# Transposing gathered rows of a mixture of experts on two 64-row tiles, up to four units at a time

## The chip, the cores and the metric

The kernel runs on one core of one Trainium2 chip. The metric is the device time of one launch in microseconds (us). The engines are named as the profile names them: PE is TensorE, DVE VectorE, ACT ScalarE, POOL GpSimd and SP SyncE.

## What is computed

Linear attention feeds a mixture of experts:

```python
def phi(x):
    proj = np.einsum('bhsd,df->bhsf', x, w_phi)
    proj = proj - np.max(np.abs(proj), axis=-1, keepdims=True)
    return np.concatenate([np.exp(proj), np.exp(-proj)], axis=-1)
kv = np.einsum('bhsf,bhsd->bhfd', k_p, v)
z = np.sum(k_p, axis=2)
num = np.einsum('bhsf,bhfd->bhsd', q_p, kv)
den = np.einsum('bhsf,bhf->bhs', q_p, z)[..., None] + 1e-06
...
e = fresh_e if s == 0 or local_gate[b, s] < 0.5 else prev_e
h = np.maximum(x[b, s] @ w1[e], 0.0)
out[b, s] = p[e] * (h @ w2[e])
```

There are 8 batches, 8 heads, 576 positions and 64 numbers a head; `num / den` of the 8 heads side by side is the row x of 512 numbers of a token. For each of the 4608 tokens a gate picks one of 8 experts (or keeps that of the token ahead of it), and the expert is two layers, 512 to 1024 with a relu and 1024 to 512, scaled by the gate's probability p. All inputs are fp32.

## The kernel before

Up to about 290 us the kernel does the attention, batch after batch, and the gates. Rows x are written to a DRAM buffer. PE works in this stage on 64 rows or 64 columns of its array at a time, and transposes with `halves` (line 290): two transposes of 64 rows each, on row tiles 0 and 64, into two banks.

A plan is then made on DVE, POOL and PE from the counts of tokens per expert: which tokens go together. A **unit** is up to 128 tokens of one expert. A **slot** is a few units of one expert that share one load of its weights: two early slots e0 and e1 of three units, made of the tokens known early, then four quads q0 to q3 (four units), four trips t0 to t3 (three), one pair p0 (two), and shared slots d0, d1 with one unit of two experts, 64 tokens each. `moe` (line 1229) sets the order q0, t0, d0, q1, t1, q2, d1, t2, q3, t3, p0. A guarded loop behind them is not run with these inputs.

A slot's work, `slots` (line 1165), runs like this. `gather_x` (line 998) fetches each unit's 128 rows with an indirect DMA on POOL's queue into one of six buffers `xg`. `tokens` (line 1015) returns one step for each unit: four 128x128 transposes on PE (line 1034) into one PSUM bank `tr`, a copy on ACT that rounds to the first half `xhi` (line 1043), and a subtraction on DVE that leaves the second half `xlo` (line 1044). Those steps are called from within the second layer of the slot ahead, one after the first matmuls of each of its units and one after the third (lines 1145 on); a shared slot has them between its four first-layer quarters. The first layer (`layer1`, line 1071) takes eight tiles of 128 hidden numbers, each four times three matmuls (`three`, lines 1048 to 1050: hi*hi, lo*hi, hi*lo) into a PSUM tile `l1` of three buffers; relu on ACT writes `hh` (line 1093) and DVE writes what is left over, `hl` (line 1094). The second layer (line 1132) takes 24 matmuls a unit into `l2`; DVE scales to `y` (line 1153) and POOL scatters the rows to the output (line 1156). The plan's later steps (`fetch`, lines 715 to 753, with the gather `lr` by POOL at line 736, for which DVE first makes `p_rim` at line 722, and the transpose on PE at line 753) run beside e0 and e1.

A shared slot (`layer1_one`, line 1100) has tokens as rows: four quarters of 256 hidden numbers, each a matmul pair on 64 columns per expert (line 1061), a relu into `hs` (line 1122), and `turn`, two transposes with one copy (lines 1109 to 1116), four times. `hs` then stands transposed in `hh`.

Weights come by DMA on SP's queue into five raw buffers; `split` (line 947) rounds them on ACT (`whi`, line 956, 128x1024) and subtracts on DVE (`wlo`, line 959). Every engine takes its instructions in the order written; the scheduler interleaves the lists by its own estimates, except that `past` keeps a split behind the last relu. PSUM has eight banks: from e1's end on `tr` and `l2` have two each (psr), a third `tr` one (psm4), and `l1` three (psl). In the early slots `tr` is taken from the attention's pool pskv.

Of the kernel before, what the change touches and what calls it, by code (L numbers as in the profile page):

```python
# [7 lines left out]
F32 = mybir.dt.float32  # L8
F32R = mybir.dt.float32r
# [5 lines left out]
PSUM = bass.MemoryType.PSUM  # L15
# [40 lines left out]
class Kernel:  # L56
# [9 lines left out]
    def run(self):  # L66
        nc, tc, A = self.nc, self.tc, self.A
        act, dve = self.act, self.dve
        with ExitStack() as root:
# [6 lines left out]
            first = self.const.tile([128, 256], F32, name="first")  # L76
# [32 lines left out]
            n = NBP * NHP * NC  # L109
# [19 lines left out]
            p = n // 2  # L129
# [777 lines left out]
    def open_main(self, root):  # L907

        self.mxt = self.mkpool(root, "moe_x2", 1, "right")
        self.w_right = self.mkpool(root, "moe_wr", WR, "right")  # L910
        self.mx2 = self.mkpool(root, "moe_h2", 2, "right")
        self.psm4 = self.mkpool(root, "moe_ps1", 1, "right", PSUM)
        self.psl = self.mkpool(root, "moe_ps2", 3, "right", PSUM)
        self.wphases = [(self.moe_early, WE), (self.w_right, WR)]

    def open_rest(self, root):
        self.w_left = self.mkpool(root, "moe_wl", WL, "left")
        self.ml1 = self.mkpool(root, "moe_l1", 1, "left")
        self.psr = self.mkpool(root, "moe_ps3", 2, "left", PSUM)
        self.wphases = [(self.moe_early, WE), (self.w_right, WR), (self.w_left, WL)]  # L920

    def wpool(self):
# [80 lines left out]
            self.pool.indirect_dma_start(x, None, self.xs[0:s["rows"], :], bass.IndirectOffsetOnAxis(s["tok"][:, u:u + 1], 0))  # L1003
            s["xg"].append(x)

    def turned(self):

        self.trn = getattr(self, "trn", 0) + 1
        if hasattr(self, "psr") and self.trn % 3:
            return self.psr.tile([128, 4, 128], F32, name="tr")  # L1010
        if not hasattr(self, "psr") and self.trn % 3 != 2:
            return self.pskv.tile([128, 4, 128], F32, name="tr", tag="kvp")
        return self.psm4.tile([128, 4, 128], F32, name="tr")

    def tokens(self, s, late=False):

        pe, n = self.pe, s["n"]
        if "xg" not in s:
            self.gather_x(s)

        def step(k):
            if k == 0:
                p = self.mxt if n > 1 else self.ml1
                s["x"] = [p.tile([128, 4, n * 128], F32R, name=x + "1" * (n == 1)) for x in ("xhi", "xlo")]
            hi, lo = s["x"]
            t = self.turned()
            with ExitStack() as st:
                if late:
                    st.enter_context(self.here())
                elif s is self.eslots[0]:  # L1030
                    st.enter_context(self.tc.high_priority())
                    st.enter_context(self.tc.issue_after(self.last_turn.ins))
                for d in range(4):
                    pe.transpose(t[:, d, :], s["xg"][k][:, d * 128:d * 128 + 128], self.ident)
            self.parts(s, hi, lo, slice(k * 128, k * 128 + 128), t)
        return [lambda k=k: step(k) for k in range(n)]

    def parts(self, s, hi, lo, o, t):

        if len(s["ei"]) == 2:  # L1040
            self.act.copy(hi[:, :, o].bitcast(F32), t)
        else:
            self.act.copy(hi[:, :, o], t)
            self.dve.tensor_sub(lo[:, :, o], t, hi[:, :, o].bitcast(F32))  # L1044

    def three(self, o, ah, al, bh, bl, first, last):
        mm = self.pe.matmul
# [52 lines left out]
    def layer1_one(self, s, between):  # L1100

        pe, act = self.pe, self.act
        xh, xl = s["x"]
        hh, hl = s["h"] = self.hidden(1)
        hs = self.ml1.tile([128, 1024], F32, name="hs", bufs=1)
        x = slice(0, 128)

        def turn(q):
            tt = self.turned()
            for j in (0, 1):  # L1110
                f = q * 2 + j
                pe.transpose(tt[:, j, :], hs[:, f * 128:f * 128 + 128], self.ident)
            hc = slice(q * 2, q * 2 + 2)
            self.parts(s, hh[:, hc], hl[:, hc], x, tt[:, 0:2])
        for q in range(4):
            t = self.psl.tile([128, 256], F32, name="l1")
            for d in range(4):
                self.both(s, q, t, xh[:, d, x], xl[:, d, x], slice(d * 256, d * 256 + 256), d == 0, d == 3)
                if d == 0 and q == 3:
                    turn(0)  # L1120
                    turn(1)
            act.activation(hs[:, q * 256:(q + 1) * 256], t, AF.Relu)
# [42 lines left out]
    def slots(self, order, held=None, soon=(), later=()):  # L1165
        first = order[0]
        if "x" not in first:
            for f in self.tokens(first):
                f()
        self.held = first.get("asked", len(first.get("w", ())))  # L1170
        self.coming, self.loaded = list(order), getattr(self, "loaded", [])
        self.marks = {}
        for i, s in enumerate(order):
            while s.get("asked", len(s.get("w", ()))) < 8:
                self.spare()
            self.need(s, 4)
            new = order[i + 1] if i + 1 < len(order) else None
            between = []
            for x in order[i + 1:i + 3 if new and len(new["ei"]) == 2 and s["n"] > 1 else i + 2]:
                if "x" not in x:  # L1180
                    between += self.tokens(x, bool(soon) and i == 0)
# [142 lines left out]
```

## Time and profile before

| what | us |
| --- | --- |
| median of 3 runs | 763.56 (762.89 to 764.04) |
| profiled execution | 755.65 |
| its span, first to last instruction | 753.9 |
| clock granted to TensorE, share of full | 0.999 |

Rows of the timeline have the start, the busy time, the engine, the line, the operation, output from inputs and shapes; "xN" are N instructions in a row, and in brackets stands how long the engine was idle ahead of it and what released it. Rows of the grouped views have the number of instructions, their busy time in us and the mean of one in ns, then the idle time ahead of them. A row of the waits has the waiting operation, what it waited for, the total, the count and the longest. PE's matmuls overlap their neighbours, so the distance between two starts says what one costs.

### The profile page before, as it was taken

The page shows a single profiled execution, that of the slowest core. Times are in us where ns is not written, and L with a number is a line of the kernel's source. Part 1 is how long each engine was busy: PE and PEld are TensorE (multiplying, and loading weights), DVE is VectorE, ACT ScalarE, POOL GpSimd, SP SyncE. Part 2 cuts the span into 40 slices and gives each one's busy share as a digit, 9 for nine tenths or more (in the row PEclk, how much of TensorE's full clock was granted, in tenths as well). Part 3 has the DMA queues.
Part 4 walks back from the last instruction along what each step waited for, and adds up shares of the span by engine and source line. Part 5 has one row for each costly group of instructions (what it writes and reads, how often), then busy time and mean ns, then how long its engine had stood idle before and what let it go on. Part 6 is the DMA issues. An engine that isn't in the chain of part 4 may idle for free. (4 is left out here: it accounts for less than half of the span.)

```text
span 753.9 us, 21898 instructions
## 1 busy us (share of the span) xinstructions
PE 728.9 (97%) x9319; PEld 632.8 (84%) x9319; DVE 451.9 (60%) x828; ACT 341.6 (45%) x648; POOL 182.1 (24%) x306
## 2 busy tenths in 40 slices
PE   7999999999998999999999999999999999999996
PEld 6999989989897888888788975889888778888995
DVE  5888888789887886674545245435522554443512
ACT  5766657666676673323343234333312444241301
POOL 0210103410374574443302041021302202101011
PEclk9999999999999999999999999999999999999999
DMA  7755545454666741154806977245486565432110
GB/s 215 247 160 141 155 123 149 138 151 130 212 202 179 229 127 54 56 178 148 314 35 248 393 248 262 83 156 193 142 289 237 162 225 168 140 125 98 57 39 29
DMA packets 66100, 125.04 MB, mean 166 GB/s; under 512 B 7220, under 2 KB 45300, under 8 KB 65950
## 3 DMA queue, kind: packets, MB, share of 16 engines
q1 hardware_dynamic: 57808, 101.03, 41.8%
q0 software_dynamic: 8016, 22.51, 8.7%
q8 instruction: 74, 1.21, 0.7%
q14 instruction: 26, 0.21, 0.1%
q10 hardware_dynamic: 176, 0.07, 0.0%
HBM read 102.05 MB, written 22.06 MB: 165 GB/s over the span
## 5 line engine op out<-in xcount | busy, mean ns | idle before, releaser
L1093 ACT ACTIVATE hh<-l 128x384 fp32r<-128x384 f32 (+1 forms) x84 | 45.2, 538 | 191.6 <-PE l L1050 191.6
L956 ACT CAST whi<-wraw 128x1024 fp32r<-128x1024 f32 x88 | 91.2, 1048 | 74.8 <-PE l L1050 42.4
L1049 PE MATMUL l<-xlo,whi 128*128 128x384 f32 (+2 forms) x352 | 123.6, 351 | 0.9 <-DVE xlo L1044 0.9
L1048 PE MATMUL l<-xhi,whi 128*128 128x384 f32 (+2 forms) x352 | 124.1, 353 | 0.0
L1050 PE MATMUL l<-xhi,wlo 128*128 128x384 f32 (+2 forms) x352 | 123.5, 351 | 0.0
L1094 DVE SCALAR_TENSOR_TENSOR hl<-l,hh 128x384 fp32r<-128x384 f32 (+1 forms) x84 | 51.6, 614 | 117.3 <-ACT hh L1093 117.2
L1048 PE MATMUL l<-whi,hh 128*128 128x512 f32 x288 | 116.8, 406 | 0.6 <-DVE y L1153 0.6
L1050 PE MATMUL l<-whi,hl 128*128 128x512 f32 x288 | 113.8, 395 | 0.0
L1049 PE MATMUL l<-wlo,hh 128*128 128x512 f32 x288 | 113.7, 395 | 0.0
L959 DVE TENSOR_TENSOR wlo<-wraw,whi 128x1024 fp32r<-128x1024 f32 x80 | 96.7, 1222 | 25.4 <-ACT whi L956 25.4
L285 ACT ACTIVATE kp<-sb 128x512 f32<-128x512 f32 x144 | 83.5, 625 | 58.7 <-DVE sb L281 56.9
L279 DVE TENSOR_REDUCE m<-pj 128x8 f32<-128x1024 f32 x72 | 87.8, 1219 | 34.0 <-PE pj L276 32.2
L276 PE MATMUL pj<-first,kq 64*128 64x128 f32 x1152 | 85.3, 289 | 7.6 <-DMA kq<-in_kqT 4.1
L281 DVE TENSOR_TENSOR sb<-pj,m 128x1024 f32<-128x1024 f32 x72 | 88.1, 1223 | 3.5
L309 ACT ACTIVATE qp<-pj 128x512 f32<-128x512 f32 x144 | 79.7, 594 | 23.1 <-PE pj L294 10.8
L404 PE MATMUL nm<-kvs,qp 128*64 128x74 f32 x2304 | 86.9, 228 | 1.4 <-ACT kvs L384 1.3
L276 PEld LDWEIGHTS pj<-first,kq 64*128 64x128 f32 x1152 | 71.5, 191 | 14.7 <-ACT ks L373 5.5
L404 PEld LDWEIGHTS nm<-kvs,qp 128*64 128x64 f32 x2304 | 79.5, 136 | 2.2 <-ACT kvs L384 1.7
L326 PE MATMUL kvp<-v,kp 128*64 128x65 f32 x2048 | 77.5, 225 | 1.3 <-issue 0.6
L1156 POOL DMA_INDIRECT out<-y,p_tokm x30 | 35.9, 1198 | 174.7 <-DVE y L1153 159.4
L1048 PEld LDWEIGHTS l<-xhi,whi 128*128 128x128 f32 x352 | 66.2, 188 | 7.5 <-issue 1.6
L326 PEld LDWEIGHTS kvp<-v,kp 128*64 128x64 f32 x2048 | 67.0, 137 | 5.7 <-ACT kp L285 1.8
(222 smaller groups left out, 923.8 us busy)
## 6 DMA issues: line engine op xcount, KB each, us to landing
wraw<-in_w1h SPq DMA_DIRECT2D x44, 512.0 KB, 5.0
wraw<-in_w2h SPq DMA_DIRECT2D x44, 512.0 KB, 5.1
kq<-in_kqT SPq DMA_DIRECT2D x47, 384.0 KB, 4.0
v<-in_va SPq DMA_DIRECT2D x48, 195.0 KB, 3.6
xs<-xo SPq DMA_DIRECT2D x48, 128.0 KB, 2.8
whi<-in_w1h SPq DMA_DIRECT2D x8, 512.0 KB
wlo<-in_w1h SPq DMA_DIRECT2D x8, 512.0 KB, 4.8
whi<-in_w2h SPq DMA_DIRECT2D x8, 512.0 KB
```

The source lines that it names most:

```text
L276: self.last_pe = self.pe.matmul(t[:, h, i % 2, j, :], kq[r, j, s], self.w2[r], start=True, stop=True)
L279: dve.tensor_reduce(m, f, AX.X, ALU.max, apply_absolute_value=True)
L281: self.last_dve = dve.tensor_sub(sb.rearrange("p h c j f -> p (h c j) f"), f, m.unsqueeze(2).broadcast_to([128, 8, 128]))
L285: self.last_act = act.activation(kp[:, :, :, sg, :].rearrange("p c h f -> p h c f"), sb[:, :, :, 0], AF.Exp, scale=1.0 - 2 * sg)
L309: self.act.activation(qp[:, sg].rearrange("p h (c r k) -> p (h c) r k", c=2, r=2), src, AF.Exp, scale=1.0 - 2 * sg)
L326: self.pe.matmul(t[r, sg, h], kp[:, h, sg, r], v[:, h], start=first and sg + h == 0, stop=last and sg + h == 2)
L404: self.last_num = self.pe.matmul(e["t"][r, c - c0, k], self.ch[i]["qp"][:, sg, h, q0 + r.start:q0 + r.stop], kvs[:, sg, k], start=sg == 0, ...
L956: self.act.copy(hi, raw)
L959: (low or self.dve).tensor_sub(lo[:, c], raw[:, c], hi.bitcast(F32)[:, c])
L1048: mm(o, ah, bh, start=first, stop=False)
L1049: mm(o, ah, bl, start=False, stop=False)
L1050: self.last_pe = mm(o, al, bh, start=False, stop=last)
```

## The change

Row tiles: where `turned` gave one bank for four 128x128 transposes, `halfbanks` gives two banks, and `rows` does eight transposes of 64 rows by 128 columns each, alternately on row tile 0 and row tile 64, one bank for each. `unrow` copies both banks with one ACT copy and one DVE subtraction of 512 columns.

Groups: `tokens` now takes the list of slots and returns steps of four units, in order (two where `late`, for e1 and q0). All transposes of a step stand next to each other on PE, then follow its copies. So e1 has a group of two and a single, q0 two pairs, t0 three, d0 with q1's first three units four, q1's last unit one, t1 three, q2 four, d1 with t2 four, q3 four, t3 three, p0 two. e0 and the single of e1 keep 128x128 transposes (`whole`). In the early slots a pair of units takes two separate banks of pskv, and `unrow` makes four copies and four subtractions of 64 tokens for two units.

Shared slots: `turn` does eight transposes of 64 rows for four tiles of `hs` and one copy of 512 columns, two times instead of four.

PSUM: the psm4 and psl pools are closed after e1, and `moe` runs with two `l1` buffers and with two `tr` tiles of two banks each, in psr and pst.

```diff
             def ahead():
-                m.append(self.tokens(self.by_size[4][0], True))
+                m.extend(self.tokens([self.by_size[4][0]], True))
...
-                       later=[[listed], [no, no] + [lambda k=k: m[0][k]() for k in range(4)]])
+                       later=[[listed], [no, no, lambda: m[0](), no, lambda: m[1]()]])
             back.close()
+            self.mid.close()
...
+        self.psl = self.mkpool(root, "moe_ps4", 2, "right", PSUM)
+        self.pst = self.mkpool(root, "moe_ps5", 1, "right", PSUM)
...
-    def turned(self):
+    def halfbanks(self):
 
         self.trn = getattr(self, "trn", 0) + 1
...
+        if not hasattr(self, "psr"):
+            return [self.pskv.tile([128, 512], F32, name="tr", tag="kvp") for _ in (0, 1)]
+        return (self.psr if self.trn % 2 else self.pst).tile([128, 2, 512], F32, name="tr", bufs=1)
...
+    def tokens(self, slots, late=False):
...
+        units, g = [(s, k) for s in slots for k in range(s["n"])], 2 if late else 4
+
+        def step(group):
+            if late and len(group) == 1:
+                self.whole(*group[0], True, self.here())
+                return
+            out = []
+            for n, (s, k) in enumerate(group):
+                if n % 2 == 0:
+                    t = self.halfbanks()
+                c = slice(n % 2 * 256, n % 2 * 256 + 256)
+                out.append((s, k, [x[:, c] for x in t] if isinstance(t, list) else t[:, :, c]))
+                with self.here() if late else nullcontext():
+                    self.rows(out[-1][2], s["xg"][k])
+            for s, k, t in out:
+                self.unrow(s, *self.into(s), k * 128, t)
+        return [lambda a=a: step(units[a:a + g]) for a in range(0, len(units), g)]
+
+    def rows(self, t, src):
+
+        for d in range(4):
+            for r in (0, 1):
+                k = slice(64 * r, 64 * r + 64)
+                o = t[r] if isinstance(t, list) else t[:, r]
+                self.pe.transpose(o[:, d * 64:d * 64 + 64], src[k, d * 128:d * 128 + 128], self.ident[k, k])
+
+    def unrow(self, s, hi, lo, at, t):
+
+        if isinstance(t, list):
+            for r in (0, 1):
+                self.parts(s, hi, lo, slice(at + 64 * r, at + 64 * r + 64), t[r].rearrange("p (d k) -> p d k", k=64))
+            return
+        hi, lo = [x[:, :, at:at + 128].rearrange("p d (r k) -> p d r k", r=2) for x in (hi, lo)]
+        self.parts(s, hi, lo, slice(0, 64), t.rearrange("p r (d k) -> p d r k", k=64))
...
         def turn(q):
-            tt = self.turned()
-            for j in (0, 1):
-                f = q * 2 + j
-                pe.transpose(tt[:, j, :], hs[:, f * 128:f * 128 + 128], self.ident)
-            hc = slice(q * 2, q * 2 + 2)
-            self.parts(s, hh[:, hc], hl[:, hc], x, tt[:, 0:2])
+            t = self.halfbanks()[:, :, 0:256]
+            self.rows(t, hs[:, q * 512:q * 512 + 512])
+            hc = slice(q * 4, q * 4 + 4)
+            self.unrow(s, hh[:, hc], hl[:, hc], 0, t)
...
                 if d == 0 and q == 3:
                     turn(0)
-                    turn(1)
...
-        def last():
-            turn(2)
-            turn(3)
-        return [last]
+        return [lambda: turn(1)]
```

What moves on the engines shows at three places. (Line numbers after the change are about 40 higher; `l_...` is a PSUM tile of a layer, with a number of its own.)

PE, the start of t0's second layer, before:

```order
L1048 MATMUL l_7603<-whi,hh 128x512
L1049 MATMUL l_7603<-wlo,hh 128x512
L1050 MATMUL l_7603<-whi,hl 128x512
L1034 MATMUL tr<-first,xg 128x128 x4
L1048 MATMUL l_7603<-whi,hh 128x512
L1049 MATMUL l_7603<-wlo,hh 128x512
L1050 MATMUL l_7603<-whi,hl 128x512
L1048 MATMUL l_7603<-whi,hh 128x512
L1049 MATMUL l_7603<-wlo,hh 128x512
L1050 MATMUL l_7603<-whi,hl 128x512
L1034 MATMUL tr<-first,xg 128x128 x4
```

and after, where lines 1091 to 1093 are the matmuls of `three` and line 1069 is the transpose of `rows`:

```order
L1091 MATMUL l_7658<-whi,hh 128x512
L1092 MATMUL l_7658<-wlo,hh 128x512
L1093 MATMUL l_7658<-whi,hl 128x512
L1069 MATMUL tr<-first,xg 128x64 x32
L1091 MATMUL l_7658<-whi,hh 128x512
L1092 MATMUL l_7658<-wlo,hh 128x512
L1093 MATMUL l_7658<-whi,hl 128x512
L1091 MATMUL l_7658<-whi,hh 128x512
L1092 MATMUL l_7658<-wlo,hh 128x512
L1093 MATMUL l_7658<-whi,hl 128x512
L1069 MATMUL tr<-first,xg 128x64 x8
```

Four units (d0 and three of q1) now stand in one block of 32 where one unit stood, and the fifth follows by itself.

DVE in e0's second layer, before; `l_6454` is the second-layer tile of e0's first unit, `wlo` and `xlo` the second halves of weights and of e1's rows, and names with `p_` belong to the plan:

```order
L959 TENSOR_TENSOR wlo<-wraw,whi 128x1024
L685 SCALAR_TENSOR_TENSOR p_i_6513<-p_one,p_f_6511 44x8
L822 SCALAR_TENSOR_TENSOR p_cm_6517<-p_f_6511,consts,p_cm_6498 44x8
L822 SCALAR_TENSOR_TENSOR p_im_6515<-p_i_6513,consts,p_im_6496 44x8
L692 TENSOR_TENSOR p_pl_6519<-p_f_6511,p_i_6513 44x8
L1153 TENSOR_SCALAR y<-l_6454,p_probe 128x512
L693 TENSOR_SCALAR p_pl_6519<-p_pl_6519 44x8
L1044 TENSOR_TENSOR xlo<-tr,xhi 128x4x128
```

and after:

```order
L1087 TENSOR_TENSOR xlo<-tr,xhi 128x4x64
L686 SCALAR_TENSOR_TENSOR p_i_6513<-p_one,p_f_6511 44x8
L823 SCALAR_TENSOR_TENSOR p_cm_6517<-p_f_6511,consts,p_cm_6498 44x8
L823 SCALAR_TENSOR_TENSOR p_im_6515<-p_i_6513,consts,p_im_6496 44x8
L693 TENSOR_TENSOR p_pl_6519<-p_f_6511,p_i_6513 44x8
L963 TENSOR_TENSOR wlo<-wraw,whi 128x1024
L694 TENSOR_SCALAR p_pl_6519<-p_pl_6519 44x8
L963 TENSOR_TENSOR wlo<-wraw,whi 128x1024
L695 TENSOR_TENSOR p_pl_6519<-p_pl_6519,p_f_6511 44x8
L963 TENSOR_TENSOR wlo<-wraw,whi 128x1024
L839 TENSOR_SCALAR p_pl_6519<-p_pl_6519 44x8
L1190 TENSOR_SCALAR y<-l_6454,p_probe 128x512
```

The halves of `xlo` now stand ahead of the three `wlo` and of `y`; before, the three `wlo` came first and a whole `xlo` stood behind `y`.

DVE at the end of e1's second layer, before q0 begins; `l_6955` and `l_7011` are second-layer tiles of e1, and `l_7082` and `l_7126` first-layer tiles of q0. Before:

```order
L959 TENSOR_TENSOR wlo<-wraw,whi 128x1024
L1153 TENSOR_SCALAR y<-l_6955,p_probe 128x512
L959 TENSOR_TENSOR wlo<-wraw,whi 128x1024
L1044 TENSOR_TENSOR xlo<-tr,xhi 128x4x128
L959 TENSOR_TENSOR wlo<-wraw,whi 128x1024
L1044 TENSOR_TENSOR xlo<-tr,xhi 128x4x128
L1153 TENSOR_SCALAR y<-l_7011,p_probe 128x512
L1094 SCALAR_TENSOR_TENSOR hl<-l_7082,hh 128x512
```

and after:

```order
L963 TENSOR_TENSOR wlo<-wraw,whi 128x1024
L1190 TENSOR_SCALAR y<-l_6967,p_probe 128x512
L963 TENSOR_TENSOR wlo<-wraw,whi 128x1024 x2
L1087 TENSOR_TENSOR xlo<-tr,xhi 128x4x64 x4
L1190 TENSOR_SCALAR y<-l_7035,p_probe 128x512
L1137 SCALAR_TENSOR_TENSOR hl<-l_7126,hh 128x512
```

One whole `xlo` stood behind the last `wlo`; now four halves stand there.

More of the change, by code (lines that the diff above doesn't have):

```diff
@@ L1004, in gather_x @@
             s["xg"].append(x)
-    def turned(self):
+    def halfbanks(self):
         self.trn = getattr(self, "trn", 0) + 1
[L1009 to L1036, printed above, removed]
@@ new lines, in halfbanks, with into, first_tokens @@
+        if not hasattr(self, "psr"):
+            return [self.pskv.tile([128, 512], F32, name="tr", tag="kvp") for _ in (0, 1)]
+        return (self.psr if self.trn % 2 else self.pst).tile([128, 2, 512], F32, name="tr", bufs=1)
+    def into(self, s):
+        if "x" not in s:
+            p = self.mxt if s["n"] > 1 else self.ml1
+            s["x"] = [p.tile([128, 4, s["n"] * 128], F32R, name=x + "1" * (s["n"] == 1)) for x in ("xhi", "xlo")]
+        return s["x"]
+    def first_tokens(self, s):
+        for k in range(s["n"]):
+            st = ExitStack()
+            st.enter_context(self.tc.high_priority())
+            st.enter_context(self.tc.issue_after(self.last_turn.ins))
+            self.whole(s, k, k == 1, st)
@@ new lines, in whole @@
+    def whole(self, s, k, alone, order):
+        hi, lo = self.into(s)
+        t = self.psm4.tile([128, 4, 128], F32, name="tr") if alone else self.pskv.tile([128, 4, 128], F32, name="tr", tag="kvp")
+        with order:
+            for d in range(4):
+                self.pe.transpose(t[:, d, :], s["xg"][k][:, d * 128:d * 128 + 128], self.ident)
+        self.parts(s, hi, lo, slice(k * 128, k * 128 + 128), t)
+    def tokens(self, slots, late=False):
+        for s in slots:
+            if "xg" not in s:
+                self.gather_x(s)
+        units, g = [(s, k) for s in slots for k in range(s["n"])], 2 if late else 4
[14 more added lines that the diff above has]
+        return [lambda a=a: step(units[a:a + g]) for a in range(0, len(units), g)]
@@ L1167, in slots @@
         if "x" not in first:
-            for f in self.tokens(first):
-                f()
+            if first is self.eslots[0]:
+                self.first_tokens(first)
+            else:
+                for f in self.tokens([first]):
+                    f()
         self.held = first.get("asked", len(first.get("w", ())))
@@ L1177, in slots @@
             new = order[i + 1] if i + 1 < len(order) else None
[L1178 to L1181, printed above, removed]
+            ahead = order[i + 1:i + 3 if new and len(new["ei"]) == 2 and s["n"] > 1 else i + 2]
+            between = self.tokens([x for x in ahead if "x" not in x], bool(soon) and i == 0)
             if s["n"] > 1:
```

13 lines of the change are left out of this document (8 added, 5 removed).

## Prediction

> **What bounds the kernel now.** I read the page first, then the waits of TensorE (PE) from the first expert slot on. The page's line of busy time:
>
> ```profile
> PE 728.9 (97%) x9319; PEld 632.8 (84%) x9319; DVE 451.9 (60%) x828; ACT 341.6 (45%) x648; POOL 182.1 (24%) x306
> ```
>
> PE's waits from 294 us to the end, with total, count and longest:
>
> ```profile
> PE l L1049 <- DVE xlo L1044: 0.9, 1, 0.9
> PE pt L753 <- issue: 0.9, 1, 0.9
> PE l L1048 <- DVE y L1153: 0.6, 1, 0.6
> PE l L1061 <- ACT hh L1041: 0.6, 1, 0.6
> ```
>
> There are four, 3.0 us together, in 459 us. So PE sets the end. What shortens its own instruction stream is gained, unless a wait takes its place; ACT's and DVE's time counts only where PE waits for them. The four places are where the cover has already run out, so there I follow each engine's order.
>
> **The transposes.** A unit's four old transposes lie between 512-column matmuls (start, busy time):
>
> ```profile
> 319.33 0.40 PE L1049 MATMUL l<-wlo,hh 128*128 128x512 f32 x1
> 319.57 0.39 PE L1050 MATMUL l<-whi,hl 128*128 128x512 f32 x1
> 319.80 0.60 PE L1034 MATMUL tr<-first,xg 128*128 128x128 f32 x4
> 320.15 0.48 PE L1048 MATMUL l<-whi,hh 128*128 128x512 f32 x1
> 320.47 0.39 PE L1049 MATMUL l<-wlo,hh 128*128 128x512 f32 x1
> ```
>
> Matmuls start 0.235 apart (319.33 to 319.80 is two). From 319.57 to 320.47 pass 0.90; less two matmuls, 0.43 belongs to the unit. I use 0.437, the same difference before rounding.
>
> The new transpose is not new: the first stage runs the same operation, 64 rows by 128 columns on two row tiles. A row of the timeline and the one of the grouped view:
>
> ```profile
> 104.47 0.41 PE L294 MATMUL pj<-first,sb 64*128 64x64 f32 x8
> ```
>
> ```profile
> L294 PE MATMUL pj<-first,sb 64*128 64x64 f32 x576 | 30.1, 223 | 3.1 <-DVE sb L281 2.7
> ```
>
> Eight last 0.41 and one lasts 0.223, so three steps from pair to pair take 0.19, 0.062 each. A unit is four pairs: 0.25 against 0.437.
>
> The price is the change of array shape, paid on entry and exit. The nearest row in a 384-column stream is a 9-row transpose:
>
> ```profile
> 305.30 0.34 PE L1050 MATMUL l<-xhi,wlo 128*128 128x384 f32 x1
> 305.57 0.23 PE L614 MATMUL pt<-first,g_ef 9*128 9x9 f32 x1
> 305.72 0.44 PE L1048 MATMUL l<-xhi,whi 128*128 128x384 f32 x1
> 306.00 0.34 PE L1049 MATMUL l<-xlo,whi 128*128 128x384 f32 x1
> ```
>
> 0.70 passes from 305.30 to 306.00, where two matmuls (0.235 x 384/512 = 0.175 each) would take 0.35. The rest, 0.35, is both switches with hardly any work. The Trainium skill, "TensorEngine Tiling (Array Packing)", section Key Properties, says that a change of tiling mode drains TensorE, which speaks against this change; it has no figure. By that rule alone a switch costs something; the row says 0.35 a round trip.
>
> A group of g units then costs 0.25g + 0.35 against 0.437g: -0.40 for four, -0.21 for three, -0.03 for two, +0.16 for one. Between 0 and 0.7 (twice the row, should a full stream drain longer than 9 rows), I take the row. On the path stand four groups of four (d0 with q1's first three; q2; d1 with t2; q3), three of three (t0, t1, t3), q1's single and p0's pair: -1.60 - 0.64 + 0.16 - 0.03 = **-2.11**. Groups of e1 and q0 lie ahead of PE waits and are put at nothing, since those waits swallow them; without that cover they would give 0.1.
>
> In the shared slots both kernels switch, as their matmuls are 64 columns wide:
>
> ```profile
> 456.75 0.38 PE L1061 MATMUL l<-wlo,xhi 128*64 128x256 f32 x1
> 457.06 0.66 PE L1112 MATMUL tr<-first,hs 128*128 128x128 f32 x4
> 457.65 0.43 PE L1061 MATMUL l<-whi,xhi 128*64 128x256 f32 x1
> 457.66 0.43 PE L1061 MATMUL l<-wlo,xhi 128*64 128x256 f32 x1
> 457.92 0.38 PE L1061 MATMUL l<-whi,xhi 128*64 128x256 f32 x1
> ```
>
> 1.17 from 456.75 to 457.92 less two pairs at 0.215 is 0.74 for four. Two such sets a slot become eight row-tile transposes each, 0.437 - 0.25 = 0.19 less; the switch stays.
>
> **e0's second layer (DVE, POOL).** e1's units come in halves of 64 tokens here. DVE's rows, then POOL's gather for the plan, then PE's transpose of what it brings:
>
> ```profile
> 326.09 0.74 DVE L1153 TENSOR_SCALAR y<-l,p_probe 128x512 f32<-128x512 f32 x1
> ...
> 332.77 0.75 DVE L1153 TENSOR_SCALAR y<-l,p_probe 128x512 f32<-128x512 f32 x1 [0.41 <-PE l L1050]
> 333.44 0.20 DVE L853 SCALAR_TENSOR_TENSOR p_km<-p_jm,table,p_km 44x1 f32<-44x1 f32 x1
> ```
>
> ```profile
> 333.80 0.98 POOL L1156 DMA_INDIRECT out<-y,p_toke  x1 [2.58 <-DVE p_km L853]
> 335.09 0.95 POOL L736 DMA_INDIRECT lr<-lst,p_rim  x1 [0.30 <-issue]
> ```
>
> ```profile
> 340.54 0.39 PE L753 MATMUL pt<-first,lr 48*128 48x48 f32 x2 [0.87 <-issue]
> ```
>
> PE already waits for the y at 326.09 (0.6 above). Now the halves stand ahead of it: three xlo halves at about 0.36 (half of a whole one's 0.68, below, and a little for starting twice) are 1.1, and the last waits some 0.35 for its ACT copy behind a weight cast. So y, and PE, come 1.45 later. But the plan's last steps now run ahead of the third y on DVE, and its gather ahead of the third output on POOL, so it can start about 1.4 earlier and L753's 0.87 vanishes: +1.45 - 0.87 = **+0.58**. Bounds: -1.4 if DVE does not fall behind and the later stages gain the gather's lead, +1.45 if the gather gains nothing.
>
> **q0's start (ACT, DVE).** Rows of the three engines:
>
> ```profile
> 367.24 1.05 ACT L956 CAST whi<-wraw 128x1024 fp32r<-128x1024 f32 x1 [2.54 <-DMA wraw<-in_w2h]
> ```
>
> ```profile
> 369.46 0.68 DVE L1044 TENSOR_TENSOR xlo<-tr,xhi 128x512 fp32r<-128x512 f32 x1
> ```
>
> ```profile
> 370.20 0.50 PE L1049 MATMUL l<-xlo,whi 128*128 128x512 f32 x1 [0.88 <-DVE xlo L1044]
> ```
>
> The last cast waits for its weights, and only xlo of one unit follows. Now four half subtractions follow that same cast: 4 x 0.36 = 1.45 instead of 0.70 until PE goes on (369.46 to 370.20 less the handover), **+0.75**. It is 0 if the halves run before the cast's weights land, and 1.5 if the four ACT copies stand in the chain too.
>
> **Two first-layer banks instead of three.** A tile's relu (ACT) and low part (DVE), 384 and 512 columns:
>
> ```profile
> L1093 ACT ACTIVATE hh<-l 128x384 fp32r<-128x384 f32 x48 | 23.6, 492 | 95.0 <-PE l L1050 95.0
> L1093 ACT ACTIVATE hh<-l 128x512 fp32r<-128x512 f32 x36 | 21.6, 600 | 96.7 <-PE l L1050 96.7
> ```
>
> ```profile
> L1094 DVE SCALAR_TENSOR_TENSOR hl<-l,hh 128x384 fp32r<-128x384 f32 x48 | 26.7, 556 | 53.0 <-ACT hh L1093 52.8
> L1094 DVE SCALAR_TENSOR_TENSOR hl<-l,hh 128x512 fp32r<-128x512 f32 x36 | 24.9, 691 | 64.4 <-ACT hh L1093 64.4
> ```
>
> Together 1.05 and 1.29, while PE works 12 x 0.175 = 2.1 or 12 x 0.235 = 2.8 on the next tile: 1.0 us or more to spare, cost nothing; one cast (1.05) in between uses it up, two would show. In the shared slot d1 it fails:
>
> ```profile
> 598.06 1.04 ACT L956 CAST whi<-wraw 128x1024 fp32r<-128x1024 f32 x1 [3.71 <-DMA wraw<-in_w2h]
> 599.01 0.38 ACT L1122 ACTIVATE hs<-l 128x256 f32<-128x256 f32 x1
> ```
>
> ```profile
> 598.10 0.38 PE L1061 MATMUL l<-whi,xhi 128*64 128x256 f32 x1
> ```
>
> The first quarter's relu sits behind a cast whose weights land at 598.06 and ends at 599.39. PE begins the third quarter at 598.10, in the third bank; with two it waits until about 599.45, +1.35. Two cheaper sets of transposes, 2 x 0.19, bring **+0.97**. Before, no wait stood here: 0 if the weights land 1.3 us sooner, one us more for each that they land later.
>
> **The copies of d0.** One 512-column copy replaces two of 256 columns, and PE waits for the first (0.6 above):
>
> ```profile
> L1041 ACT COPY hh<-tr 128x256 f32<-128x256 f32 x8 | 2.6, 373 | 0.0
> L1041 ACT COPY xhi<-tr 128x512 f32<-128x512 f32 x2 | 1.2, 583 | 0.6 <-PE tr L1034 0.6
> ```
>
> +0.21; the cheaper transposes go into that wait. Gathers of later units (POOL) run up to six units ahead; I find no PE wait on them and put a group's later release at nothing. If that cover goes, a gather's landing of some microseconds shows.
>
> **Sum.** -2.11 + 0.58 + 0.75 + 0.97 + 0.21 = +0.40 on the profiled execution's own 755.65: 756.05. The median of the runs shown is 763.56, 1% above that execution; the sum has no reason to scale, so 763.56 + 0.40 = **764.0**. A measurement of this kernel tells about 0.2%, 1.5 us, from no change.
>
> **Rivals.** *B, the new waits dissolve* (faster). Each of the three costs rests on weights that land when they landed before. The order of loads on SP is the same, but buffers come free at other times; if the halves run earlier and d1's weights land 1.3 us sooner, 0.75, 0.58 and 1.35 go and -2.11 - 0.38 + 0.21 = -2.3 is left: 761.3. For it: all three are single events. Against: PE itself arrives sooner, which makes waits on DMA longer. 0.20.
>
> *C, no drain* (faster). If the two shapes overlap without the 0.35, nine groups on the path give 3.15 more: +0.40 - 3.15 = -2.75, 760.8. Against it is the 9-row transpose and the shared slot (0.74 for what costs 0.437 elsewhere). 0.06.
>
> *D, two banks behind an in-order ACT* (slower). Its place is the shared slots, its price one us of PE for each us that d1's cast of second-layer weights is held. PE reaches d1 about 1 us sooner relative to the transfers, and a raw buffer freed a cast later delays the load by about 1.05: 0.40 + 1.0 + 1.05 = +2.4, 766.0. It decides once the landing is over 1.1 us later against PE than before. The idle of 3.71 before that cast speaks for it. 0.25.
>
> *E, the groups are split again on PE.* The order shows 32 transposes in one row, so 0.02; about 763.6.
>
> My forecast holds 0.47. Within 0.2%: 0.47 + 0.02 = 0.49; faster B + C = 0.26; slower D = 0.25. The range 761.0 to 766.0 takes B's own value and D's to its price; beyond lie C and the tails of B and D, 0.06 + 0.06 + 0.08.
>
> **What would show it.** Right: a group of four units takes 1.35 us of PE; the third quarter of d1 waits about 1.3 us for ACT; PE waits about 1.6 for xlo at q0; the wait of L753 is gone and one for y has grown to 2. Wrong: a group of four at 1.0 or less (C) or above 1.75 (the twice-dear switch), d1 without a wait (B), or a wait on first-layer banks in quads and trips, which I put at nothing.

## The result and the profile after

The changed kernel takes 768.65 us (768.03 to 769.14, six runs) against 763.09 us of the kernel before: a ratio of 1.0077, 95% interval 1.0060 to 1.0094. It is slower by 5.6 us; the forecast was 764.0 with a range of 761.0 to 766.0. The profiled execution took 768.65 as well, with a span of 766.9. The page's line of busy time, and the waits of TensorE (PE) in the expert slots, to be laid beside those of before:

```profile
PE 732.9 (96%) x9471; PEld 632.0 (82%) x9471; DVE 451.7 (59%) x834; ACT 341.3 (45%) x650; POOL 182.1 (24%) x306
```

```profile
PE l L1091 <- DVE y L1190: 4.2, 1, 4.2
PE l L1091 <- ACT xhi L1086: 3.5, 2, 1.9
PE l L1104 <- ACT hh L1084: 1.9, 2, 1.4
PE l L1104 <- ACT hs L1162: 1.0, 1, 1.0
```

The four waits of 0.6 to 0.9 us have become six, of 10.6 us together. First what came out as forecast, a group of four units on PE in t0's second layer:

```profile
446.04 0.40 PE L1093 MATMUL l<-whi,hl 128*128 128x512 f32 x1
446.37 1.21 PE L1069 MATMUL tr<-first,xg 64*128 64x64 f32 x32
447.51 0.50 PE L1091 MATMUL l<-whi,hh 128*128 128x512 f32 x1
447.85 0.40 PE L1092 MATMUL l<-wlo,hh 128*128 128x512 f32 x1
```

From 446.04 to 447.85 pass 1.81; less two matmuls at 0.235, the four units cost 1.34, where the prediction had 1.35 and the old transposes 1.75.

Then where the time went. e0's second layer: PE's transposes of e1's pair, ACT's copies of them, DVE's subtraction and the y behind it, and PE again:

```profile
318.61 0.71 PE L1069 MATMUL tr<-first,xg 64*128 64x64 f32 x16
```

```profile
316.39 2.93 ACT L960 CAST whi<-wraw 128x1024 fp32r<-128x1024 f32 x3
325.31 0.65 ACT L1086 CAST xhi<-tr 128x256 fp32r<-128x256 f32 x2 [5.99 <-PE tr L1037]
```

```profile
325.71 0.42 DVE L1087 TENSOR_TENSOR xlo<-tr,xhi 128x256 fp32r<-128x256 f32 x1 [4.94 <-ACT xhi L1086]
...
335.12 0.74 DVE L1190 TENSOR_SCALAR y<-l,p_probe 128x512 f32<-128x512 f32 x1
```

```profile
335.92 0.79 PE L1091 MATMUL l<-whi,hh 128*128 128x512 f32 x1 [4.19 <-DVE y L1190]
```

The transposes are over by 319.32 and ACT has been free since 319.3, but its first copy runs at 325.31: PE's signal reached it 6 us late. (The copy waits for the pair alone: in a later profile of the same program, below, it runs at 317.57, before the third unit's transposes of L1037. That the profile names L1037 only means that L1037 was the last to signal before the copy ran.) DVE takes its work in order, so it stands still for 4.94 us, with the plan's steps, three weight subtractions and y queued behind the first half. y runs at 335.12 and PE, with both its second-layer tiles full, waits for it. The clock then adds its part. Columns of the next view: the stretch; its length and the busy time of PE, PEld, DVE, ACT and POOL; the granted clock; DMA share and GB/s:

```profile
335.00:340.00 5.00, 4.08 (x10) 3.21 (x11) 4.93 (x24) 1.05 (x1) 2.06 (x2) 0.51 0.91 337
340.00:345.00 5.00, 5.00 (x21) 4.15 (x20) 1.29 (x6) 0.00 (x0) 0.94 (x1) 0.81 0.63 173
```

The granted clock was 0.51 in the first 5 us and 0.81 in the next; less the 0.9 us in which PE still waited, some 3 us of matmul time are lost. The Trainium skill, "TensorE: Matmul & The Clock Gate", section "What's actually happening", says that the array goes back to half rate after at least one idle window of about 3.4 us; the trace agrees in kind (0.51 after a wait of 4.2 us). It does not need an idle stretch as long as that, though: a wait of 2.36 us was enough in a second profile of before (below).

### The profile page after: what moved, and what is told of

The parts are those of the page before. It is cut to its first block, busy times and chain, and to the rows that moved or that the text cites. A ratio compares the mean times of both kernels' runs of the same rounds, so it can differ in the third digit from the quotient of the medians.

```text
span 766.9 us, 22217 instructions
## 1 busy us (share of the span) xinstructions
PE 732.9 (96%) x9471; PEld 632.0 (82%) x9471; DVE 451.7 (59%) x834; ACT 341.3 (45%) x650; POOL 182.1 (24%) x306
## 5 line engine op out<-in xcount | busy, mean ns | idle before, releaser
L405 PE MATMUL nm<-kvs,qp 128*64 128x74 f32 x2304 | 88.5, 228 | 2.1 <-issue 0.9
```

The costliest lines, as they stand in the source:

```text
L405: self.last_num = self.pe.matmul(e["t"][r, c - c0, k], self.ch[i]["qp"][:, sg, h, q0 + r.start:q0 + r.stop], kvs[:, sg, k], start=sg == 0, ...
```

## The experiments

Times of before differed between the four sets of runs (763.35, 757.51, 762.51 and 757.62), so that each ratio holds within its set.

**Before once more.** The kernel unchanged, for a second profile.

> The kernel before once more, for a second profile. Theory 1 (the early slots hold the loss): no wait of TensorE over 1 us after 294 us, and the attention ends within 1 us of either profile. Rival (the first profile was a lucky execution: 755.65 against a median of 763): a wait of 3 to 5 us and a lower granted clock between 320 and 390 us here too, and a span near 761.

763.68 us, span 761.9, against 753.9 in the first profile. PE's longest wait, ACT's copies of e1's first two units, and the stretch behind the wait:

```profile
PE l L1048 <- DVE y L1153: 2.4, 1, 2.4
```

```profile
320.98 0.59 ACT L1043 CAST xhi<-tr 128x512 fp32r<-128x512 f32 x1 [0.19 <-issue]
325.11 1.05 ACT L956 CAST whi<-wraw 128x1024 fp32r<-128x1024 f32 x1 [3.54 <-DMA wraw<-in_w1h]
326.95 0.59 ACT L1043 CAST xhi<-tr 128x512 fp32r<-128x512 f32 x1 [0.79 <-remote]
```

```profile
333.00:338.00 5.00, 4.58 (x13) 3.63 (x14) 4.93 (x20) 1.04 (x1) 3.14 (x3) 0.66 0.65 245
```

The rival holds in the main: the profile on which the prediction stands was a lucky execution. (The wait is 2.4 us where the rival had 3 to 5.) Usually the kernel before has late signals too, a wait for y of 2.4 in place of 0.65, and a drop of the clock behind it. They are not only signals from PE to ACT (the second unit was transposed by 325.2 and copied at 326.95). DVE also waits for its own earlier steps, four times and 1.6 us in all, where the first profile has no idle time; one of the four:

```profile
326.02 0.16 DVE L778 TENSOR_SCALAR p_th<-p_r 44x8 int32<-44x8 int32 x1 [0.47 <-DVE p_bef L822]
```

The copy of the first unit, on which DVE and the plan hang, was in time: transposed by 320.59 (the block starts at 319.99 and takes 0.60), copied at 320.98. And of the 8.0 us between the two profiles only 3.3 lie in e0's second layer; 4.8 lie ahead of it, in the attention (the relu of e0's eighth tile starts at 317.47 against 312.65).

**Which part loses.** late_whole gives e1's and q0's units back their single 128x128 transposes; early_rows is the kernel before with only those units in pairs; two_banks is the kernel before with two first-layer banks from q0 on.

```diff
# late_whole, on the changed kernel (and q0's four steps called one by one)
-        units, g = [(s, k) for s in slots for k in range(s["n"])], 2 if late else 4
+        units, g = [(s, k) for s in slots for k in range(s["n"])], 1 if late else 4
...
-            if late and len(group) == 1:
-                self.whole(*group[0], True, self.here())
+            if late:
+                self.whole(*group[0], group[0][1] % 3 == 1, self.here())
# early_rows, on the kernel before: in tokens; pairs() holds the changed kernel's late steps
+        if late:
+            return self.pairs(s)
# two_banks, on the kernel before: in open_rest, the old psm4 and psl closed ahead of it
+        self.psm4 = self.mkpool(root, "moe_ps4", 1, "right", PSUM)
+        self.psl = self.mkpool(root, "moe_ps5", 2, "right", PSUM)
```

> The changed kernel with e1's and q0's units transposed one by one as 128x128 again, all else as changed. Theory 1 (the paired row tiles of the early slots hold the loss, since DVE stands still behind their first half with the plan queued behind it): 760.5 to 763, the wait for y at e0's second layer falls from 4.2 us to under 1. Rival 2 (the two first-layer banks and the shared slots hold it): 767 to 769, no change. Rival 3 (a stall that comes with any new program): the wait for y stays over 3 us.

> The kernel before with only e1's and q0's units in paired row tiles and copies of 64 tokens; the main part and its banks as before. Theory 1: 768 to 772, with the wait for y of 4 us. Rival 2: 763 to 764.5. Rival 3: anything, and no tie to the row tiles.

> The kernel before with two first-layer banks instead of three from q0 on, and nothing else. Theory 1: the two shared slots pay 1 us each, 764.5 to 765.5. Rival 2: 767 to 769. By my prediction's own terms: 1.35 us in d1 and 0.1 in d0, 764.5.

late_whole 762.57, ratio 0.9995 (0.9979 to 1.0012). early_rows 768.59, 1.0079 (1.0051 to 1.0108). two_banks 763.79, 1.0014 (0.9995 to 1.0032). The pairs of the early slots are the whole loss, and everything else in the change adds up to nothing that stands clear of the interval. In early_rows the wait for y is 4.2 us; in late_whole it is 2.5, as in before's second profile, and not under 1 as expected. Two banks alone cost 0.4 us by the medians, under the 764.5 that was expected, but the interval holds both that and nothing. They show one new wait, in d1, at the place and nearly of the size that was forecast (1.35):

```profile
606.06 0.43 PE L1065 MATMUL l<-whi,xhi 128*64 128x256 f32 x1 [1.12 <-ACT hs L1126]
```

**Place or halves.** single_first transposes e1's first unit alone and pairs the other two; late_copy leaves the pair's transposes where they are and writes its copies behind the third unit's; pair_first moves the pair ahead of the plan's counting on PE.

```diff
# single_first
+        cut = [0, 1, 3] if late and len(units) == 3 else list(range(0, len(units), g)) + [len(units)]
+        return [lambda a=a, b=b: step(units[a:b]) for a, b in zip(cut, cut[1:])]
# late_copy
-            for s, k, t in out:
-                self.unrow(s, *self.into(s), k * 128, t)
...
+            if late and len(units) == 3:
+                return copies
...
+            def last():
+                step(units[2:])
+                wait[0]()
+            return [lambda: wait.append(step(units[:2])), last]
# pair_first
-                rest = list(later[i]) + rest
+                rest = rest[:1] + list(later[i]) + rest[1:] if i == 0 else list(later[i]) + rest
```

> The changed kernel, but of e1's three units the first is transposed alone (128x128) and the second and third as the pair; q0 stays in pairs. Theory A (a late signal: the pair's end reaches ACT 6 us late because it falls into the stretch in which the plan's scatters and the next weights move, and DVE stands still with the plan queued behind it): the first unit's signal gets out ahead of that stretch, the wait for y falls from 4.2 to about 2.5 us, 763 to 765.5 (q0's pairs still cost). Theory B (the halves themselves, four copies and four subtractions, hold it): 768 to 769.

> The changed kernel with e1's pair transposed where it was, but its copies and subtractions written behind those of e1's third unit, so that DVE has the plan and y of e0 ahead of them. Theory A: DVE no longer stands behind the late signal, the wait for y falls under 2.5 us, 762.5 to 765.5. Theory B: the same halves still run before e1 begins, 767 to 769. Theory C (row-tiled transposes in this stage hold up TensorE itself): 768 to 769.

> The changed kernel with e1's pair transposed three matmuls into e0's second layer, ahead of the plan's counting instead of behind it. Theory A: the signal gets out ahead of the scatters' stretch, ACT copies within 1 us of the transposes, 763 to 766 (the plan starts 0.7 us later). Theory B or C: 768 to 770.

single_first 758.78, ratio 1.0015 (0.9992 to 1.0038); late_copy 758.37, 1.0014 (0.9995 to 1.0032); pair_first 756.81, 0.9986 (0.9965 to 1.0006). All three lie with before, whose time in this set was 757.51; the times expected were for a before of 763. But in the profiled executions of this set no signal was late, and the changed kernel did not run beside them, so the set alone does not decide. The next one does: the changed kernel and late_copy together, where signals are late.

> The changed kernel once more, beside other kernels. Theory A (the signal of e1's pair comes late on some executions only: where it does, the wait for y is 4 us and the time 1.0077 of before; where no signal is late, the cost is my prediction's own terms): either 1.006 to 1.009 with the wait of 4 us, or 1.000 to 1.003 with a wait for y of about 1 to 1.5 us and all copies within 1 us of their transposes. Theory B (the halves themselves): 1.006 or more whether or not a signal is late.

> late_copy once more beside the changed kernel itself. Theory A: if the changed kernel loses 5 us or more here, this one loses 2 at most, since DVE does not stand behind the late signal; if the changed kernel loses nothing here, both lie within 1.5 us. Theory C (row tiles hold up TensorE): both lose alike.

The changed kernel 766.97, 1.0059 (1.0032 to 1.0085), with the late signal and a wait for y of 4.2; late_copy 760.62, 0.9979 (0.9957 to 1.0000). late_copy's transposes of the pair, ACT's copies, and PE's longest waits:

```profile
320.03 0.71 PE L1081 MATMUL tr<-first,xg 64*128 64x64 f32 x16
```

```profile
326.69 0.65 ACT L1098 CAST xhi<-tr 128x256 fp32r<-128x256 f32 x2 [5.95 <-PE tr L1037]
```

```profile
PE l L1103 <- ACT xhi L1098: 2.2, 1, 2.2
PE l L1116 <- ACT hh L1096: 1.9, 3, 1.1
PE l L1103 <- DVE y L1202: 1.1, 1, 1.1
```

These rows settle it between the three theories. The signal is as late as in the changed kernel (5.95 us), and the four halves are all there. Only their place has changed, in DVE's order and for the last two copies in ACT's, and the wait for y is 1.1 instead of 4.2. Theory B (the halves) and theory C (row tiles that hold up TensorE) fall: the loss is what was queued behind the late signal.

They do not show why this signal is late, and the place of the pair, as theory A has it, does not explain it. Here the pair is over by 320.74, 3.3 us after the start of e0's eighth relu (317.43), and waits until 326.69. In before's second profile the single unit was over by 320.59, 3.1 us after that relu (317.47), and was copied at 320.98. That two units or row tiles make the signal late is a rival which these two rows speak for and no run here settles.

**Three banks.** late_whole with three first-layer banks and one pair of transposing banks.

```diff
-        self.psl = self.mkpool(root, "moe_ps4", 2, "right", PSUM)
-        self.pst = self.mkpool(root, "moe_ps5", 1, "right", PSUM)
+        self.psl = self.mkpool(root, "moe_ps4", 3, "right", PSUM)
...
-        return (self.psr if self.trn % 2 else self.pst).tile([128, 2, 512], F32, name="tr", bufs=1)
+        return self.psr.tile([128, 2, 512], F32, name="tr", bufs=1)
```

> The changed kernel with e1's and q0's units one by one as 128x128 (as in late_whole, 762.6) and three first-layer banks, with one pair of transposing banks instead of two. By the sum of the groups, -2.1, and the shared slots' cheaper sets, -0.4, without the waits for banks (1.3 us in late_whole): 760.5 to 761.5, ratio 0.996 to 0.998. Rival: the single pair of transposing banks makes the second half of each group of four wait for ACT's copy and costs 0.5 to 1 us a group, 763 to 766.

761.37, ratio 1.0046 (1.0024 to 1.0067): slower, as the rival had it. The wait of PE's matmuls for hs is gone, but PE waits four times for hh, 3.4 us in all, in the shared slots. That the second set of transposes there needs the pair of banks which the first set's copy still holds is the likely reason, argued only. The groups pay in another way than by a wait. Where late_whole has 32 transposes in a row in t0's second layer, this kernel has two blocks of 16 (they begin at 434.70 and 437.62) with matmuls between them, and all seven groups of three and four are split so. At the 0.35 that the prediction has for a change of shape and back, that is some 2.5 us, an estimate.

**q0, and banks in halves.** pair_first_q0w is pair_first with q0's units one by one; half_quarters adds to it that two quarters of a shared slot use the halves of one bank.

```diff
# q0's units one by one
+        g = (1 if len(units) == 4 else 2) if late else 4
# half_quarters
-            t = self.psl.tile([128, 256], F32, name="l1")
+            if q % 2 == 0:
+                two = self.psl.tile([128, 512], F32, name="l1")
+            t = two[:, q % 2 * 256:q % 2 * 256 + 256]
```

> The changed kernel with e1's pair ahead of the plan's counting (as in pair_first) and q0's units one by one as 128x128. If q0's pairs cost the wait for xhi at q0's start and the clock's drop behind it (2.5 us and 1.7 us in pair_first), 0.993 to 0.996 of before. If they cost only what before already waited there (0.9 us), 0.997 to 0.999.

> As pair_first_q0w, and in the shared slots two quarters share one first-layer bank (256 columns each), so that four quarters fit in two banks. If the wait for a bank is what d0 and d1 pay (1.2 us for hs in d1), 1.0 to 1.5 us less than pair_first_q0w. If a relu that reads one half of a bank holds up the writing of the other half, 0 to 2 us more.

pair_first_q0w 760.30, ratio 0.9976 (0.9959 to 0.9992); half_quarters 762.16, 0.9999 (0.9981 to 1.0017). The first beats before, by what the second of its two expectations had: PE's wait for xlo at q0 is 0.9 us again, as before. It also shows a pair ahead of the counting in an execution with late signals. The pair is over by 318.19 and ACT is free from 319.26:

```profile
321.09 0.65 ACT L1087 CAST xhi<-tr 128x256 fp32r<-128x256 f32 x2 [1.83 <-PE pt L764]
```

So the signal did not come within 1 us, as theory A had expected of pair_first; it was 2.9 us late, and the late copy did less harm there. Half banks cost 1.9 us. In d1 PE's second quarter waits 1.6 us until the relu of the first has read the other half of the bank (PE goes on at 608.46, the relu ends at 608.41), in place of 1.2 for the third quarter. So the writing of one half was held up until the other was read; the wait is one on ACT's signal, and whether the hardware would need it is not shown. A second wait, of 1.7 us in d0, is of transposes which need the relu's output itself.

**A last set, beside the changed kernel.** pair_whole transposes e1's first two units as 128x128, eight in one block at the pair's place; after_q0w changes q0 alone; late_copy_q0w joins late_copy and q0's single units.

```diff
# pair_whole
+            if late and len(units) == 3:
...
+                for t, (s, k) in zip(ts, group):
+                    with self.here():
+                        for d in range(4):
+                            self.pe.transpose(t[:, d, :], s["xg"][k][:, d * 128:d * 128 + 128], self.ident)
+                for t, (s, k) in zip(ts, group):
+                    self.parts(s, hi, lo, slice(k * 128, k * 128 + 128), t)
```

> The changed kernel as the reference on this chip for the three beside it: 1.005 to 1.009 of before where the pair's signal is late (wait for y about 4 us), 1.000 to 1.003 where it is not.

> The changed kernel with e1's first two units as 128x128 transposes, eight in one block at the pair's place, copies behind both, 512 columns each; the rest as changed. If the row tiles or the copies of 64 tokens make the signal late or dear: 1.000 to 1.003, wait for y under 3 us. If the place does it (two units in one block end later, and all copies wait for a signal of that stretch): the signal is late here too, the wait for y stays at 3.5 to 4.5 us and the time within 1.5 us of the changed kernel.

> The changed kernel with only q0's units one by one as 128x128; e1's pair stays. If q0's pairs cost what the trace shows at q0's start (waits of 2.8 to 3.5 us in place of 0.7 to 0.9): 2 us less than the changed kernel, 1.003 to 1.006. If e1's pair alone makes the loss: 1.006 to 1.009, as the changed kernel.

> late_copy (e1's pair where it was, its copies behind the third unit's) with q0's units one by one as 128x128. By the terms seen so far: the groups' -2.1, the shared slots +0.6 together, no loss in the early slots, 1.5 to 2 us less at q0 than late_copy: 0.995 to 0.998 of before, the same as or faster than pair_first_q0w (0.9976).

The changed kernel 761.32, 1.0047 (1.0020 to 1.0073); pair_whole 758.69, 1.0014 (0.9994 to 1.0034); after_q0w 759.38, 1.0015 (0.9993 to 1.0037); late_copy_q0w 755.96, 0.9971 (0.9955 to 0.9988). So q0's pairs are about 2 us of the loss here (761.32 less 759.38; the intervals overlap), and late_copy_q0w is faster than both kernels; what is left on its PE:

```profile
PE l L1117 <- ACT hh L1097: 1.7, 2, 1.2
PE l L1105 <- DVE xlo L1100: 0.9, 1, 0.9
```

pair_whole is 2.6 us faster than the changed kernel, but in its profiled execution no signal was late. So it does not tell whether row tiles make the signal of that stretch later than 128x128 transposes would.

The changed kernel's own profile in this set is worth as much as any edit, for it shows the same program where the signal is not late. It shows the fastest of nine executions (757.51 against a median of 761.32). PE, ACT, and PE's longest waits:

```profile
316.76 0.71 PE L1069 MATMUL tr<-first,xg 64*128 64x64 f32 x16
```

```profile
317.57 0.65 ACT L1086 CAST xhi<-tr 128x256 fp32r<-128x256 f32 x2
```

```profile
PE l L1091 <- ACT xhi L1086: 2.3, 1, 2.3
PE l L1091 <- DVE y L1190: 1.9, 1, 1.9
PE l L1104 <- ACT hh L1084: 1.4, 2, 0.9
```

The copies follow the transposes within 0.1 us, the clock does not drop, and the wait for y is 1.9, close to the 2 that the prediction named. The span is 755.7.

## Why the prediction was wrong, point by point

The table has the time from one relu to the next milestone, in us, in five profiles: before (the prediction's), before once more, the changed kernel, the changed kernel again (beside late_copy), and the changed kernel without the late signal. Each number is the distance between the starts of two relu rows.

| stretch | before | before, again | changed | changed, again | changed, no late signal | forecast of the change |
| --- | --- | --- | --- | --- | --- | --- |
| e0's 8th tile to e1's 1st | 22.03 | 25.29 | 30.46 | 29.68 | 23.29 | |
| e1's 1st to its 5th (the plan's transpose) | 9.43 | 9.11 | 8.50 | 8.50 | 8.50 | both: +0.58 |
| e1's 5th to q0's 1st | 28.92 | 28.54 | 31.38 | 29.03 | 30.30 | +0.75 |
| q0's 1st to q1's 1st (d0) | 97.65 | 97.70 | 98.47 | 98.50 | 97.99 | -0.24 |
| q1's 1st to p0's last (d1) | 266.27 | 266.55 | 265.17 | 265.21 | 264.58 | -0.68 |

- **The step that failed** is the term of e0's second layer, +0.58 with bounds of -1.4 and +1.45, and the sentence that carried it to the runs: "the sum has no reason to scale". The term took it that ACT copies the pair as soon as its own casts let it ("the last waits some 0.35 for its ACT copy behind a weight cast"). In the runs the first copy came 6 us after the transposes, with DVE and the plan queued behind it. Between executions with late signals the first two rows of the table give +4.6 (30.46 + 8.50 less 25.29 + 9.11), and +3.8 in the changed kernel's second such profile. Of the 4.6, y is 4.0 later (it starts 19.12 after e0's eighth relu instead of 15.16) and a longer drop of the clock is some 1.3; 0.6 that the gather gains comes off.
- **The sign that was there.** The runs were 8 us longer than the profile, so they held something which the profile did not show. Late signals in e0's second layer and the clock's drop are 3.3 of it; the other 4.8, in the attention, have no part in the change.
- **Against the like profile** the sum comes out, in part by luck. 755.7 is 1.8 above 753.9, and of that 1.5 lies in the attention, which the change does not touch (e0's 8th tile begins at 314.16 against 312.65). The five stretches of the table make +0.36 where the sum had +0.40, but out of +0.33, +1.38, +0.34 and -1.69 for the forecast's +0.58, +0.75, -0.24 and -0.68.
- **The mechanism at e0** was right as far as it went: halves ahead of y on DVE. "y, and PE, come 1.45 later" was 1.2 without a late signal (the y begins 14.65 after e0's 8th relu instead of 13.44), and L753's wait is gone. But nothing bounded what a wait would cost that is new on DVE with a whole plan behind it.
- **q0's start** was mis-sized and moves between executions: +0.75 forecast; +0.5 and +2.8 with late signals, +1.4 without. Of the 2.8, some 1.7 is a drop of the clock behind PE's wait of 1.85 us, which the prediction did not have:

```profile
380.00:385.00 5.00, 3.54 (x10) 2.65 (x11) 2.42 (x6) 0.70 (x2) 1.01 (x1) 0.78 1.00 391
385.00:390.00 5.00, 5.00 (x20) 4.06 (x20) 0.96 (x2) 1.20 (x2) 0.00 (x0) 0.87 0.29 114
```

  What its upper end named, "if the four ACT copies stand in the chain too", did come. (The 2.8 and 3.5 us in the expectation of after_q0w are sums of two waits each; at q0 stand 1.0 and 1.9.) The copies of the changed kernel and PE's start:

```profile
378.99 0.64 ACT L1086 CAST xhi<-tr 128x256 fp32r<-128x256 f32 x2
380.71 0.70 ACT L1086 CAST xhi<-tr 128x256 fp32r<-128x256 f32 x2 [1.08 <-DVE xlo L1087]
```

```profile
381.46 0.51 PE L1091 MATMUL l<-xhi,whi 128*128 128x512 f32 x1 [1.85 <-ACT xhi L1086]
```

  The third copy waits for DVE's subtraction of the first, which waits for the weights' subtraction, so ACT and DVE take turns, which a whole unit's single copy did not.
- **The transposes** were right in size: 1.34 for four, and by the same distances 1.08 for three and 0.59 for one.
- **d1** was right in mechanism and too dear: a wait of 1.0 and 1.1 us for the bank came with late signals, and one of 0.2 without, and the stretch from q1 on gained 1.4 us, 0.7 more than forecast.
- **d0** was too cheap, +0.21 against +0.8 to +1.2 (its row of the table, less the groups' -0.45). The wide second copy was meant to cost only its width. It stands behind two casts on ACT which wait for the next weights; ACT and PE after, then ACT before:

```profile
474.59 1.04 ACT L960 CAST whi<-wraw 128x1024 fp32r<-128x1024 f32 x1 [0.67 <-DMA wraw<-in_w1h]
476.52 1.04 ACT L960 CAST whi<-wraw 128x1024 fp32r<-128x1024 f32 x1 [0.89 <-DMA wraw<-in_w1h]
477.48 0.58 ACT L1084 COPY hh<-tr 128x512 f32<-128x512 f32 x1
```

```profile
478.11 0.64 PE L1104 MATMUL l<-whi,hh 128*64 128x512 f32 x1 [1.35 <-ACT hh L1084]
```

```profile
461.73 1.05 ACT L956 CAST whi<-wraw 128x1024 fp32r<-128x1024 f32 x1 [0.48 <-DMA wraw<-in_w1h]
462.68 0.64 ACT L1041 COPY hh<-tr 128x256 f32<-128x256 f32 x2
```

- **The rivals.** C fell: the switch costs what the 9-row transpose said. B did not come in the runs. E fell: 32 transposes stand in a row. D had the right kind of cause, an in-order engine that stands behind a late arrival, at the wrong place: it was the early slots and DVE, not the shared slots and ACT, which late_whole shows (762.57 with the shared slots as changed).

## What to carry to other kernels

When the runs are longer than the profiled execution by more than the effect in question, take a second profile before forecasting: the first may lack a wait that the change will feel. An in-order engine pays for the wait of the first instruction in its queue with everything behind it, so a copy that waits for another engine belongs behind the work that others need, even when it takes little time itself. Joining small steps into a block moves every copy to the block's end: ask what each engine had between them.

## What the runs showed of the hardware that was not expected

- Signals came late in one stretch of some 6 us in e0's second layer, in all profiled executions of the first and third sets and in the changed kernel's first, with and without the change, and in none of the second and fourth. From PE to ACT it was up to 6 us, for the pair; DVE waited up to 1.09 us for its own step ahead (late_copy_b):

```profile
326.57 0.17 DVE L779 TENSOR_SCALAR p_th<-p_r 44x8 int32<-44x8 int32 x1 [1.09 <-DVE p_bef L823]
```

  It is the stretch in which POOL's nine scatters of the plan run and the next weights begin to load. But these alone do not make it: in both profiles of before the nine scatters run from 3.7 us ahead of e0's eighth relu to 7.8 behind it and SP asks for the next weights 3.2 behind it, and in the first no signal is late. Why some executions are spared was not found; neither the scatters nor the loads were taken away.
- A change of the array's shape and back costs about 0.35 us around blocks of one, three and four units: 1.34 for four, 1.08 for three and 0.59 for one, a step of 0.25 a unit, and the rest is the switch.
- The granted clock fell to half for 3.4 us (a mean of 0.66 over 5 us) after a wait of PE of 2.36 us in before's second profile. In the changed kernel's it did so for 6.8 us after a wait of 4.19 (0.51 and 0.81 over 5 us each) and for some 3.5 us after one of 1.85 (0.78 and 0.87). It did not fall after waits of 2.3 and 1.9 us in the profile without late signals, so the length of the wait alone does not decide it.
